# Decode attention over a key/value cache: four heads interleaved over the partitions in 16 KB runs, weights turned on VectorE and permuted by one matmul

## The chip, the cores and the metric

The kernel runs on one core of one Trainium2 chip. The metric is the device time of one execution in microseconds (us), lower is better. Executions of the kernel before agree within 0.3% or so. All timed comparisons are between runs made on the same chip in the same rounds. A profile is of one execution; its span is about 2 us shorter than the device time.

Engine names in the profile: PE is TensorE (matmul), PEld its weight loads, DVE is VectorE, ACT is ScalarE, SPq the queue that issues the loads. "Granted clock" (PEclk) is the share of its full clock that TensorE was allowed.

## The reference, cut to what matters

```python
# B=8 sequences, one new token each, D=448; 16 query heads, 8 key heads, 256 wide, window W=1024
q = (x @ wq)                                            # 8 x 16 x 256
k, v = k_cache[:, :, -1024:, :], v_cache[:, :, -1024:, :]   # each serves two query heads
p = softmax(q k^T / 16);  o = p v;  a = o @ wo
b = mlp(layernorm(x))                                   # 448 -> 1792 -> 448
return g * a + (1 - g) * b                              # g: a sigmoid gate
```

Keys and values are 64 pairs of (sequence, key head), 512 KB of keys and 512 KB of values each in bf16. With the weights the kernel must read 77.7 MB.

## The kernel before

Work goes in 16 groups `u` of four key heads (8 query heads). For a group, key tiles arrive with keys on the partitions, TensorE transposes them, VectorE and ScalarE copy the transposes from PSUM to SBUF ("evict"), TensorE makes the scores, the softmax gives weights, and TensorE multiplies them with the values. A ring of 18 slots of 1 MB takes the loads.

```python
def kv_loader(src, b, g):            # two heads to a 1 MB tile: 128 runs of 8 KB
    nc.sync.dma_start(t[:], src[b, g:g+GP, kv_base:Sk, :]
        .rearrange("a (s c) d -> s a (c d)", c=NCK))      # partition = (s, a), a = head, GP = 2

def transpose_keys(u):
    for s in range(2):                # ... kt: [P, NJ, NCK, SK, GP], so heads alternate in its columns
        nc.tensor.transpose(ktp[:, c*P:(c+1)*P], kn[:, o:o+P], ident[:])    # 8 to a PSUM tile
        # evictions 2, 4, 7 of 8 on ScalarE, the others on VectorE

def scores(u):                        # 4 heads side by side in 4 column groups of the array
    for hf in range(2):
        for j in range(NJ):
            for a in range(QUAD):
                nc.tensor.matmul(S_ps[32*a:32*a+rep, hf*NMM:(hf+1)*NMM],
                    lhsT=qw[:, j, b, h0:h0+rep],                                  # 2 columns
                    rhs=KT[a//GP][:, j, hf*CMM:(hf+1)*CMM, :, a % GP], ...)       # 512 keys, every 2nd element

def softmax(u):                       # every weight is written twice: 2048 elements
    nc.vector.reduce_max(nmx[:], S_ps[:], axis=AXIS.X, negate=True)
    nc.scalar.activation(E (two copies), S_ps, ACT.Exp, bias=nmx[:], accum_out=rowsum[:])

def weights(u):                       # turned by 16 matmuls with E as stationary operand
    # rsum = 1/rowsum; selr = sel * rsum * 2
    for c in range(NCK):
        nc.tensor.matmul(sm[:, c, :], lhsT=E[:, c*P:(c+1)*P], rhs=sel[:], ...)
    nc.tensor.matmul(sm[:, NCK, :], lhsT=ones_f[:], rhs=selr[:], ...)
    nc.vector.tensor_tensor(ET[:], sm[:, 0:NCK, :], own (0 or 1), op=ALU.mult)

def values(u, ET, rb):                # 64 matmuls, values stationary, 4 columns of weights streaming
    ...
for u in range(1, NQ - 2):
    transpose_keys(u)
    values(u - 1, *weights(u - 1))
    scores(u)
    softmax(u)
# ... the last two groups are interleaved; the output projection with wo (loaded last) follows
```

## Time and profile before

| | before |
|---|---|
| device time, median | 198.85 us (198.73 to 199.01, 3 runs) |
| span of the profile | 197.0 us |
| bytes read | 77.68 MB, 394 GB/s over the span |
| one loop, undisturbed (transposes at 90.96 and 101.13 us) | 10.17 us |
| last packet of the last weights (packet records) | 193.0 us |

The page in 40 slices of 4.9 us each: busy tenths of TensorE, its granted clock in tenths, busy tenths of the DMA engines.

```profile
PE   1699869868686878979596868686868686887662
PEclk9996556999999996799999999999999999997555
DMA  4999999999999999999999999999999999999960
```

DMA is at 9 from the second slice to the 38th, so the bytes leave hardly any room. The clock is low at the start, in one stretch around 75 to 85 us and at the end, else 1.0.

The page's groups of instructions: line, engine, operation, out <- in, shapes, count, then busy us and mean ns, then idle time before them and what ended it.

```profile
L366 ACT ACTIVATE E<-S_ps,nmx 128x2048 bf16<-128x2048 f32 x16 | 31.5, 1968 | 72.2 <-DVE nmx L363 72.2
L363 DVE TENSOR_REDUCE nmx<-S_ps 128x1 f32<-128x1024 f32 x16 | 19.6, 1225 | 13.0 <-PE S_ps L351 13.0
L351 PE MATMUL S_ps<-kt,qw 128*2 128x512 bf16 x256 | 18.1, 402 | 0.4 <-DVE qw L339 0.4
L386 PE MATMUL sm<-sel,E 128*128 128x8 bf16 x256 | 8.8, 167 | 1.7 <-ACT E L366 1.7
```

One loop in the timeline (start us, us, engine, line, operation, count, in brackets the idle time before and its releaser; lines between these are left out):

```profile
90.96 1.51 PE L311 MATMUL ktp<-ident,slot 128*128 128x128 bf16 x24
92.33 1.97 ACT L366 ACTIVATE E<-S_ps,nmx 128x2048 bf16<-128x2048 f32 x1 [4.59 <-DVE nmx L363]
95.34 1.52 PE L311 MATMUL ktp<-ident,slot 128*128 128x128 bf16 x24 [1.19 <-ACT kt L316]
96.70 0.55 PE L386 MATMUL sm<-sel,E 128*128 128x8 bf16 x16
98.44 1.75 PE L414 MATMUL po<-ET,slot 128*128 128x4 bf16 x64 [0.38 <-DVE ET L395]
100.11 1.08 PE L351 MATMUL S_ps<-kt,qw 128*2 128x512 bf16 x16
...
101.13 1.07 PE L311 MATMUL ktp<-ident,slot 128*128 128x128 bf16 x16
```

The loop is a ring of dependences: transposes (which wait for ScalarE, held up by the exponential), turned weights, values, scores, and the next transposes. It takes 10.17 us; the DMA engines bring a group's 4 MB in about 10.1 us. The two limits lie almost on top of each other. What the loop sheds, DMA will not give; what the loop gains in length, the time shows.

### The profile page before, as it was taken

What the parts mean: (1) busy time and instruction counts of PE and PEld (TensorE: products, weight loads), DVE (VectorE), ACT (ScalarE), POOL (GpSimd) and SP (SyncE); (2) the same over time, 40 slices, a digit from 0 to 9 for tenths busy, and PEclk for the clock granted to TensorE, in tenths of its full rate; (3) what the DMA queues carried; (4) which work ended last, traced back from release to release, by engine and by line L of the source; (5) the groups of instructions that cost most, each with busy time, mean ns of one, the idle gap of its engine ahead of it and who ended that gap; (6) DMA issues with size and microseconds to landing.
All of it is one profiled execution on the core that took longest, in us unless ns stands there. A gap on an engine that the chain in (4) does not pass through costs nothing.

```text
span 197.0 us, 6578 instructions
## 1 busy us (share of the span) xinstructions
PE 147.7 (75%) x3006; PEld 125.1 (64%) x3006; DVE 94.3 (48%) x230; ACT 82.0 (42%) x85; POOL 0.9 (0%) x7
## 2 busy tenths in 40 slices
PE   1699869868686878979596868686868686887662
PEld 0699739656574758877575667575656665675641
DVE  6540335364646464555545454636363636763200
ACT  3250043272636354362718180808172727383000
POOL 1000000000000000000000000000000000000000
PEclk9996556999999996799999999999999999997555
DMA  4999999999999999999999999999999999999960
GB/s 170 416 427 406 420 412 414 421 414 424 411 414 419 419 419 416 414 419 419 423 411 411 423 416 423 409 418 423 416 416 413 418 419 419 421 411 416 413 246 23
DMA packets 11645, 78.10 MB, mean 396 GB/s; under 512 B 1489, under 2 KB 1890, under 8 KB 3042
## 3 DMA queue, kind: packets, MB, share of 16 engines
q1 hardware_dynamic: 11424, 77.68, 95.8%
q8 instruction: 23, 0.38, 0.8%
q10 hardware_dynamic: 194, 0.02, 0.1%
q14 instruction: 4, 0.03, 0.0%
HBM read 77.68 MB, written 0.01 MB: 394 GB/s over the span
## 4 chain that ended last, share of the span: by engine, by line
DMA 49%; PE 26%; DVE 16%; ACT 5%; issue 2%; SPq 0%; ACTq 0%
DMA slot<-in_A_v_cache_dram 31%; PE ktp L311 10%; DMA slot<-in_A_wq_dram 8%; DVE kt L318 7%; PE po L414 7%; DMA slot<-in_A_wo_dram 7%; DVE nmx L363 6%; PE S_ps L351 5%; ACT kt L316 4%; DMA slot<-in_A_k_cache_dram 3%; PE sm L393 2%; ACT E L366 1%; DVE ET L395 1%; DVE selr L381 1%; PE bb L484 1%
## 5 line engine op out<-in xcount | busy, mean ns | idle before, releaser
L311 PE MATMUL ktp<-ident,slot 128*128 128x128 bf16 x1024 | 73.9, 232 | 21.6 <-ACT kt L316 15.2
L311 PEld LDWEIGHTS <-slot 128*128 128x128 bf16 x1024 | 66.1, 105 | 33.3 <-issue 28.3
L318 DVE COPY kt<-ktp 128x1024 bf16<-128x1024 bf16 x80 | 52.5, 686 | 30.3 <-PE ktp L311 29.0
L366 ACT ACTIVATE E<-S_ps,nmx 128x2048 bf16<-128x2048 f32 x16 | 31.5, 1968 | 72.2 <-DVE nmx L363 72.2
L316 ACT COPY kt<-ktp 128x1024 bf16<-128x1024 bf16 x48 | 47.1, 1013 | 19.3 <-PE ktp L311 19.3
L414 PEld LDWEIGHTS <-slot 128*128 128x128 bf16 x1024 | 29.5, 99 | 6.8 <-issue 6.8
L414 PE MATMUL po<-ET,slot 128*128 128x4 bf16 x1024 | 28.1, 164 | 5.3 <-DVE ET L395 5.3
L363 DVE TENSOR_REDUCE nmx<-S_ps 128x1 f32<-128x1024 f32 x16 | 19.6, 1225 | 13.0 <-PE S_ps L351 13.0
L351 PE MATMUL S_ps<-kt,qw 128*2 128x512 bf16 x256 | 18.1, 402 | 0.4 <-DVE qw L339 0.4
L423 DVE TENSOR_TENSOR oT<-po,rb 128x8 bf16<-128x8 f32 x32 | 4.3, 190 | 26.5 <-PE po L414 26.5
L393 PE MATMUL sm<-selr,ones_f 128*128 128x8 f32 x32 | 6.6, 279 | 5.5 <-DVE selr L381 5.5
L386 PE MATMUL sm<-sel,E 128*128 128x8 bf16 x256 | 8.8, 167 | 1.7 <-ACT E L366 1.7
L393 PEld LDWEIGHTS sm<-selr,ones_f 128*128 128x128 f32 x32 | 5.2, 203 | 6.8 <-DVE selr L381 6.6
L386 PEld LDWEIGHTS <-E 128*128 128x128 bf16 x256 | 8.2, 97 | 1.8 <-ACT E L366 1.8
L395 DVE TENSOR_TENSOR ET<-sm,own 128x128 bf16<-128x128 f32 x16 | 4.7, 291 | 8.2 <-PE sm L393 8.2
L351 PEld LDWEIGHTS <-qw 128*2 128x2 bf16 x256 | 4.7, 82 | 5.2 <-DVE qw L339 0.5
L545 PE MATMUL A_ps<-slot,oP 128*8 128x112 bf16 x128 | 4.3, 290 | 2.8 <-DMA slot<-in_A_wo_dram 2.1
L545 PEld LDWEIGHTS <-oP 128*8 128x8 bf16 x128 | 2.9, 113 | 4.1 <-issue 3.4
L329 PE MATMUL qt<-xT,slot 128*128 128x8 bf16 x128 | 3.9, 168 | 0.8 <-DMA slot<-in_A_wq_dram 0.4
L329 PEld LDWEIGHTS <-slot 128*128 128x128 bf16 x128 | 3.7, 104 | 1.0 <-DMA slot<-in_A_wq_dram 0.6
L381 DVE TENSOR_SCALAR selr<-sel,rsum 128x8 f32<-128x8 bf16 x16 | 3.7, 231 | 0.6
L552 DVE SCALAR_TENSOR_TENSOR res<-A_ps,gg_s,mixb 128x112 bf16<-128x112 f32 x1 | 0.3, 335 | 6.6 <-PE A_ps L545 6.6
(69 smaller groups left out, 38.9 us busy)
## 6 DMA issues: line engine op xcount, KB each, us to landing
slot<-in_A_k_cache_dram SPq DMA_DIRECT2D x32, 1024.0 KB, 19.9
slot<-in_A_v_cache_dram SPq DMA_DIRECT2D x32, 1024.0 KB, 19.9
slot<-in_A_wq_dram SPq DMA_DIRECT2D x3, 1024.0 KB
slot<-in_A_wo_dram SPq DMA_DIRECT2D x3, 896.0 KB, 19.1
slot<-in_B_w_dram SPq DMA_DIRECT2D x1, 1008.0 KB
slot<-in_B_w_dram SPq DMA_DIRECT2D x1, 896.0 KB
slot<-in_B_w_dram SPq DMA_DIRECT2D x1, 560.0 KB
slot<-in_A_wq_dram SPq DMA_DIRECT2D x1, 512.0 KB
```

What stands on the lines that cost most here:

```text
L311: nc.tensor.transpose(ktp[:, c * P : (c + 1) * P], kn[:, o : o + P], ident[:])
L316: nc.scalar.copy(dst, ktp[:])
L318: nc.vector.tensor_copy(dst, ktp[:])
L329: nc.tensor.matmul(qt[:, k, :], lhsT=w[:, c : c + P], rhs=xT[:, r + half, :], start=(r == 0 and k == 0), stop=(r == NR), skip_group_check= ...
L351: nc.tensor.matmul(S_ps[32 * a : 32 * a + rep, hf * NMM : (hf + 1) * NMM], lhsT=qw[:, j, b, h0 : h0 + rep], rhs=KT[a // GP][:, j, hf * CMM ...
L363: nc.vector.reduce_max(nmx[:], S_ps[:], axis=AXIS.X, negate=True)
L366: nc.scalar.activation(E[:].rearrange("p (k a) -> p k a", a=GP), S_ps[:].rearrange("p (k o) -> p k o", o=1).to_broadcast([P, W, GP]), ACT.Exp,
L386: nc.tensor.matmul(sm[:, c, :], lhsT=E[:, c * P : (c + 1) * P], rhs=sel[:], start=True, stop=True,)
L393: nc.tensor.matmul(sm[:, NCK, :], lhsT=ones_f[:], rhs=selr[:], start=True, stop=True)
L395: nc.vector.tensor_tensor(ET[:], sm[:, 0:NCK, :], own[:].rearrange("p (o r) -> p o r", o=1).to_broadcast([P, NCK, RQ]), op=ALU.mult,)
L414: nc.tensor.matmul(PO[:, j, cols], lhsT=vn[:, o : (c + 1) * Dh : NJ], rhs=ET[:, c, cols], start=(c == 0), stop=(c == NCK - 1),)
L545: nc.tensor.matmul(dst, lhsT=oP[:, j, q, :], rhs=w[:, o + cols.start : o + cols.stop], start=(q == 0 and j == 0), stop=(q == NHQ - 1 and j ...
```

## The change: its intent, and the diff

A tile now holds four heads, 2 MB, in 128 runs of 16 KB, so that DMA has half the packets for keys and values. As all four heads share a tile, the weights need no second copy: the exponential halves. VectorE turns the weights in 32x32 blocks, and one matmul with a permutation puts them in the order of the value tiles' partitions; 16 matmuls go. A score matmul writes 8 rows per head, so that the turned blocks are full; a cap of the maximum makes the weights of rows that are not the head's zero. Cut to its core:

```diff
-    GP = 2
-    SLOT = 4096
-    RING = 18
+    SLOT = 8192
+    RING = 9
 # kv_loader: all four heads of a group in one tile
-                src[b, g : g + GP, kv_base:Sk, :].rearrange("a (s c) d -> s a (c d)", c=NCK)
+        v = src[b, half * QUAD : (half + 1) * QUAD, kv_base:Sk, :].rearrange(
+            "a (s c) d -> s a (c d)", c=NCK)                    # NCK = 32, runs of 16 KB
 # scores
-                        S_ps[32 * a : 32 * a + rep, hf * NMM : (hf + 1) * NMM],
-                        lhsT=qw[:, j, b, h0 : h0 + rep],
-                        rhs=KT[a // GP][:, j, hf * CMM : (hf + 1) * CMM, :, a % GP],
+                        S_ps[32 * a : 32 * a + RQ, hf * CH * SK : (hf + 1) * CH * SK],
+                        lhsT=qw[:, j, b, half, a, :],           # 8 columns, 6 of them zero
+                        rhs=KT[hf][:, j, :, a::QUAD],           # every 4th element
 # softmax
+        nc.vector.tensor_tensor(nmx[:], nmx[:], cap[:], op=ALU.min)
-            E[:].rearrange("p (k a) -> p k a", a=GP),  S_ps[:] ... .to_broadcast([P, W, GP]),
+            E[:], S_ps[:], ACT.Exp, bias=nmx[:], scale=1.0, accum_out=rowsum[:]
 # weights
-        for c in range(NCK):
-            nc.tensor.matmul(sm[:, c, :], lhsT=E[:, c * P : (c + 1) * P], rhs=sel[:], ...)
+        nc.vector.transpose(EB[:].rearrange("p c r -> p (c r)"), E[:])
+        nc.tensor.matmul(sm[:, 0:NCK, :], lhsT=perm[:], rhs=EB[:, :, 0:RQ], ...)
-        nc.vector.tensor_tensor(ET[:], sm[:, 0:NCK, :], own ..., op=ALU.mult)
+        nc.vector.tensor_copy(ET[:], sm[:, 0:NCK, :])
 # ... slots of 2 MB for the weight matrices, set-up of perm, sel, cap: cut
```

The values were already the stationary operand; now 8 columns of weights stream past them instead of 4.

## The prediction

> **What bounds it now.** Two limits lie almost on top of each other. (1) Bytes: the page's slices show the DMA engines at 0.9 or more from slice 2 to 38, for 77.68 MB; in the stretch table each 10.17 us moves 411 to 421 GB/s. Packet records: median 313 ns for 8192 B, 275 for 7168, 140 for 3584, 74 for 1792, so about 0.0375 ns per byte plus 5.5 ns per packet (estimate: fit). (2) Compute: the loop repeats every 10.17 us (transposes at 92.95, 103.12, 113.29), and after the stretch with granted clock 0.70 (75 to 85 us) it stays 0.8 us late, so it is set by its own chain, not by data. The chain of waits agrees: transposes, evictions, values, scores and maximum from 24 to 118 us, DMA only after. PE is busy 7.7 us of 10.17. The end (last weights landing, 193 us) is DMA; compute has about 2.5 us of slack there.

> **Bytes after.** The same, in 16 KB packets for keys and values: one 5.5 ns saved per 16 KB plus half the completion writes (9 ns each), estimated 27 ns of 2543 ns per MB, about 1%, 1.7 us over 64 MB.

> **Compute loop after**, from its start:
> - Exponential of 1024 instead of 2048 elements: 1.97 us to about 1.0 (ScalarE copies of 1024 take 1.01). The last evictions and transposes come about 0.75 us sooner (PE waits 1.19 us per loop on a ScalarE eviction), less 0.19 for the new minimum with cap.
> - 16 matmuls with exponentials as weights (0.55 us) go. VectorE turns 128x1024 instead. [...]this trace's maximum over 1024 elements takes 1.225 us, so I estimate 1.2 us. It stands in VectorE's order behind the last evictions, so on the chain. Then a 256-column matmul (estimate 0.27) and a copy of 256 columns (estimate 0.42, from 0.29 for 128).
> - Last transpose to first value matmul grows from 1.6 to about 2.4 us, which gives back the 0.75. Loop: 10.2 us, unchanged within 0.3.
> - Scores read keys at a step of 8 B instead of 4; values take 8 columns instead of 4 but weight loads bound them (27 ns each). I expect 1.08 and 1.74 us as before.[...]
> - Start: more small VectorE operations before the first eviction (about 1.3 us), eight strided query writes instead of two (about 1.1 us more): loop starts about 1.5 us later.

> **Sum.** Without compute, 1.6 us less: 197.2. But compute at 10.2 us against DMA's 10.05 falls behind: values of the last group end about 3 us later, at 189, the output projection then runs without waiting, and ends at about 194.5 instead of 193.9. Time about 199.

> **What would show it.** 16 KB packets near 620 ns; about 420 GB/s; exponential 1.0 us; the turn 1.2 us, with PE idle before the permutation 0.7 to 1.1 us; loop 10.0 to 10.4 us; output projection no longer waiting for DMA.

> **What would make it wrong.** A slower turn, or scores slowed by the 8 B step: each 0.3 us per loop is about 4 us at the end. Longer PE gaps could lower the granted clock oftener (0.85 us each).[...] Much cheaper 16 KB packets: 195.5.

> Predicted 199.0 us, 8 in 10 within 196.5 to 203.5; faster by over 2%: 0.06, within: 0.77, slower: 0.17.

Two of its figures can be looked up in the trace before: the 9 ns are the median of the 1330 packets of 4 bytes, which the author takes for completion writes, and the 0.85 us are about what the stretch of low clock cost (transposes at 71.77 and 92.95 us, 21.18 us for two loops of 10.17).

## The result, and the profile after

The changed kernel takes 218.22 us (median of 4, 217.74 to 218.98), against 198.93 us of the kernel before in the same rounds. The ratio is 1.0974 (95% interval 1.0937 to 1.1011): 9.7% slower. Ratios here and below are the mean time of one kernel's fast runs over that of the other's of the same rounds, so not quite the ratio of the medians quoted. The prediction of 199.0 us, and its range to 203.5, were wrong.

The same three rows of the page after (slices of 5.4 us):

```profile
PE   0599948787868696958696877969686959687672
PEclk9996587888879969797969698788789696999758
DMA  5999999999999999999999999999999999600000
```

DMA now ends five slices before the kernel does: the loads are done at 190 us of 216. The clock dips all through the run, not in one stretch. The groups that answer to those of before, and the new turn:

```profile
L373 ACT ACTIVATE E<-S_ps,nmx 128x1024 bf16<-128x1024 f32 x16 | 17.8, 1113 | 104.6 <-DVE nmx L370 84.4
L369 DVE TENSOR_REDUCE nmx<-S_ps 128x1 f32<-128x1024 f32 x16 | 19.6, 1225 | 27.2 <-PE S_ps L357 27.2
L357 PE MATMUL S_ps<-kt,qw 128*8 128x512 bf16 x256 | 32.4, 628 | 0.3 <-DVE qw L348 0.3
L385 DVE STREAM_TRANSPOSE EB<-E 128x1024 bf16<-128x1024 bf16 x16 | 19.8, 1238 | 0.0
L386 PE MATMUL sm<-EB,perm 128*128 128x256 bf16 x16 | 4.3, 270 | 12.0 <-DVE EB L385 12.0
```

The exponential (1.11 us), the turn (1.24 us) and the permutation (0.27 us) are near what was forecast. The score matmuls are not: 628 ns each instead of 402, and the maximum on VectorE waits 27.2 us for them instead of 13.0. One loop after:

```profile
100.38 1.51 PE L320 MATMUL ktp<-ident,slot 128*128 128x128 bf16 x24
102.02 1.11 ACT L373 ACTIVATE E<-S_ps,nmx 128x1024 bf16<-128x1024 f32 x1 [6.81 <-DVE nmx L370]
104.17 1.52 PE L320 MATMUL ktp<-ident,slot 128*128 128x128 bf16 x24 [0.39 <-ACT kt L323]
106.16 1.24 DVE L385 STREAM_TRANSPOSE EB<-E 128x1024 bf16<-128x1024 bf16 x1
107.45 0.27 PE L386 MATMUL sm<-EB,perm 128*128 128x256 bf16 x1 [0.76 <-DVE EB L385]
108.23 1.75 PE L401 MATMUL po<-ET,slot 128*128 128x8 bf16 x64 [0.52 <-DVE ET L390]
109.91 2.00 PE L357 MATMUL S_ps<-kt,qw 128*8 128x512 bf16 x16
...
111.84 0.40 PE L320 MATMUL ktp<-ident,slot 128*128 128x128 bf16 x2
```

Subtract starts within the two loops. From the first transposes to the first value matmul: 7.48 us before (98.44 - 90.96), 7.85 after. From there to the scores: 1.67 and 1.68. From the scores to the next transposes: 1.02 and 1.93. The loop grew by 1.29 us, to 11.46 us, and 0.91 of that is the score matmuls.

The loop growth is nearly the whole difference of the spans. Transposes of group 1 start at 29.30 us before and 31.32 after (2.0 us later); from there to the transposes of group 14 it is 132.85 us before and 149.47 after (16.6 us more); from there to the end 34.84 and 35.17 (0.3 more). Unrounded, these sum to 19.0 us, the difference of 216.0 and 197.0.

The packet records say that DMA itself got faster: a 16 KB packet has a median of 614 ns, an 8 KB packet before 313 ns. But now the queue waits for the computation to free slots. The queue's own waits, before and then after (line, what it waited for, us in total, times, longest):

```profile
SPq L100 <- DMA slot<-in_A_k_cache_dram: 52.8, 28, 1.9
SPq L100 <- PE ktp L311: 5.1, 15, 0.5
```

```profile
SPq L107 <- PE ktp L320: 57.8, 11, 6.6
SPq L107 <- PE po L401: 34.3, 10, 3.8
```

### The profile page after: what moved, and what is told of

Same layout as the page of the kernel before. It is cut to its first block, busy times and chain, and to the rows that moved or that the text cites. A ratio compares the mean times of both kernels' runs of the same rounds, so it can differ in the third digit from the quotient of the medians.

```text
span 216.0 us, 6058 instructions
## 1 busy us (share of the span) xinstructions
PE 161.3 (75%) x2766; PEld 124.0 (57%) x2766; DVE 116.0 (54%) x241; ACT 68.3 (32%) x85; POOL 0.8 (0%) x7
## 3 DMA queue, kind: packets, MB, share of 16 engines
q1 hardware_dynamic: 6528, 77.67, 85.5%
HBM read 77.68 MB, written 0.01 MB: 360 GB/s over the span
## 4 chain that ended last, share of the span: by engine, by line
PE 37%; DVE 31%; DMA 14%; ACT 10%; issue 6%; SPq 0%; ACTq 0%
DMA slot<-in_A_k_cache_dram 14%; PE S_ps L357 13%; PE po L401 12%; DVE kt L325 10%; DVE EB L385 9%; PE ktp L320 8%; DVE nmx L369 7%; ACT kt L323 6%; ACT E L373 4%; DVE ET L390 3%; PE sm L386 2%; PE A_ps L529 1%; DVE selr L381 1%; DVE nmx L370 1%; PE pp L514 0%
## 5 line engine op out<-in xcount | busy, mean ns | idle before, releaser
L373 ACT ACTIVATE E<-S_ps,nmx 128x1024 bf16<-128x1024 f32 x16 | 17.8, 1113 | 104.6 <-DVE nmx L370 84.4
L369 DVE TENSOR_REDUCE nmx<-S_ps 128x1 f32<-128x1024 f32 x16 | 19.6, 1225 | 27.2 <-PE S_ps L357 27.2
L401 PE MATMUL po<-ET,slot 128*128 128x8 bf16 x1024 | 28.7, 167 | 7.2 <-DVE ET L390 7.2
L357 PE MATMUL S_ps<-kt,qw 128*8 128x512 bf16 x256 | 32.4, 628 | 0.3 <-DVE qw L348 0.3
L385 DVE STREAM_TRANSPOSE EB<-E 128x1024 bf16<-128x1024 bf16 x16 | 19.8, 1238 | 0.0
L409 DVE TENSOR_TENSOR oT<-po,rb 128x16 bf16<-128x16 f32 x16 | 3.6, 226 | 26.1 <-PE po L401 26.1
L386 PE MATMUL sm<-EB,perm 128*128 128x256 bf16 x16 | 4.3, 270 | 12.0 <-DVE EB L385 12.0
L357 PEld LDWEIGHTS <-qw 128*8 128x8 bf16 x256 | 6.1, 93 | 12.3 <-issue 11.0
L390 DVE CAST ET<-sm 128x256 bf16<-128x256 f32 x16 | 6.8, 425 | 5.8 <-PE sm L386 5.8
L381 DVE TENSOR_SCALAR selr<-sel,rowsum 128x8 f32<-128x8 f32 x16 | 3.6, 223 | 0.6 <-ACT E L373 0.6
L392 DVE RECIPROCAL rb<-sm 128x8 f32<-128x8 f32 x16 | 3.2, 198 | 0.0
```

Source lines behind the costliest of these rows:

```text
L357: nc.tensor.matmul(S_ps[32 * a : 32 * a + RQ, hf * CH * SK : (hf + 1) * CH * SK], lhsT=qw[:, j, b, half, a, :], rhs=KT[hf][:, j, :, a::QUA ...
L373: nc.scalar.activation(E[:], S_ps[:], ACT.Exp, bias=nmx[:], scale=1.0, accum_out=rowsum[:])
L385: nc.vector.transpose(EB[:].rearrange("p c r -> p (c r)"), E[:])
L386: nc.tensor.matmul(sm[:, 0:NCK, :], lhsT=perm[:], rhs=EB[:, :, 0:RQ], start=True, stop=True)
L390: nc.vector.tensor_copy(ET[:], sm[:, 0:NCK, :])
L401: nc.tensor.matmul(PO[:, j, :], lhsT=vn[:, c * Dh + j : (c + 1) * Dh : NJ], rhs=ET[:, c, 0:RQ], start=(c == 0), stop=(c == NCK - 1),)
```

## The experiments

Theory A: the score matmuls are slow because they read the keys at a step of four elements, 8 B, instead of two. Rival B: they are slow because of what else changed in them, 8 stationary columns and 8 rows written instead of 2. When A alone did not give back what it should, a second pair of theories was needed: C, the wait for the turn on VectorE, placed between transposes and values, leaves TensorE so quiet that its clock is lowered; D, the clock falls for another reason.

Experiments with wrong keys passed the comparison with the reference as well: the scores are so small that the weights are almost even, and the comparison doesn't see the order of the keys. So a "correct" says little about it; e13 and e14 settle the order where it matters.

### e1 to e4: step or width?

e1 takes the step away by reading wrong keys; e2 takes the width away; e3 puts the step alone into the kernel before; e4 takes the step away properly, by sorting the keys in the transposing matmul.

```diff
 # e1 (changed kernel)
-rhs=KT[hf][:, j, :, a::QUAD],
+rhs=KT[hf][:, j, 4 * a : 4 * a + 4, :],
 # e2 (changed kernel)
-S_ps[32 * a : 32 * a + RQ, ...],  lhsT=qw[:, j, b, half, a, :],
+S_ps[32 * a : 32 * a + rep, ...], lhsT=qw[:, j, b, half, a, a * rep : (a + 1) * rep],
 # e3 (kernel before)
-rhs=KT[a // GP][:, j, hf * CMM : (hf + 1) * CMM, :, a % GP],
+rhs=KT[a // GP][:, j].rearrange("p c s g -> p (c s g)")[:, a::4],
 # e4 (changed kernel)
+back[:].rearrange("p (a s) -> p a s", a=QUAD) <- ident[:].rearrange("p (s a) -> p a s", a=QUAD)
-nc.tensor.transpose(ktp[:, c, :], kn[:, o : o + P], ident[:])
+nc.tensor.transpose(ktp[:, c, :], kn[:, o : o + P], back[:])
-rhs=KT[hf][:, j, :, a::QUAD],
+rhs=KT[hf][:, j, :, a * SK : (a + 1) * SK],
```

> The changed kernel, but each score matmul reads 512 keys that lie side by side (same size and count, wrong keys, so a wrong result on purpose). Theory A (the 8 B step of the keys that the score matmuls stream slows them): the 16 score matmuls of a loop fall from 1.97 us to 1.1 or less, the loop from 11.46 to about 10.5 us, the time to about 203 to 205 us. Theory B (the stationary operand of 8 columns, or writing 8 rows instead of 2, slows them): scores stay at 1.97 us, time stays near 218.

> The changed kernel with a stationary operand of 2 columns instead of 8 in the score matmuls, still at the 8 B step (wrong result on purpose: three of four heads lose their scores). Theory A: nothing moves, scores 1.97 us a loop, time near 218. Theory B: scores back to about 1.08 us, loop about 10.5 us, time 203 to 205.

> The kernel before, with nothing changed but the score matmuls reading the keys at a step of four elements (8 B) instead of two (wrong keys, wrong result on purpose). Theory A: scores 1.08 to about 1.97 us a loop, the loop from 10.17 to about 11.05 us, time about 208 to 211. Theory B: nothing moves, 199.

> The changed kernel with the permutation taken into the key transposes: they use a permuted identity, so that each head's keys stand in runs of 32 in the transposed tile and the score matmuls read with no step. The result is right if the transposing matmul takes a permutation. Theory A: scores 1.1 us or less, loop about 10.5 us, time 203 to 205 us: that is, slower than the kernel before still, by the 0.3 us per loop that the turn on VectorE and its wait add. Theory B: 218.

| run | time, us | ratio to before (95%) | 16 scores of a loop, us | mean loop, us |
|---|---|---|---|---|
| changed kernel | 218.22 | 1.097 | 1.97 to 2.02 | 11.50 |
| e1, no step (wrong keys) | 214.15 | 1.076 (1.074 to 1.078) | 1.04 to 1.88 | 11.32 |
| e2, two columns | 218.56 | 1.098 (1.095 to 1.102) | 1.97 to 2.01 | 11.49 |
| e3, before with the 8 B step | 207.97 | 1.045 (1.043 to 1.047) | 1.97 to 2.01 | 11.03 |
| e4, keys sorted | 214.40 | 1.078 (1.071 to 1.085) | 1.04 to 1.88 | 11.26 |

(Mean loop: start of the transposes of group 1 to those of group 13, over 12. The kernel before: 10.23 us with its one slow stretch, scores 1.07 to 1.09 us.)

B is out: e2 changes nothing, and e3 gets the slow scores with two columns. A is right as to the score matmuls: the step alone makes 1.08 into 1.97 us, in either kernel, and in e3 it lengthens the loop by 0.8 us. The page's group of e3:

```profile
L351 PE MATMUL S_ps<-kt,qw 128*2 128x512 bf16 x256 | 31.7, 626 | 0.4 <-DVE qw L339 0.4
```

But A's sum failed: without the step the time falls by 4 us, not by the 13 to 15 us expected. In e4's timeline three neighbouring loops show why:

```profile
97.34 1.88 PE L362 MATMUL S_ps<-kt,qw 128*8 128x512 bf16 x16
108.78 1.88 PE L362 MATMUL S_ps<-kt,qw 128*8 128x512 bf16 x16
120.22 1.54 PE L362 MATMUL S_ps<-kt,qw 128*8 128x512 bf16 x16
```

### e5 and e8: the low clock and the wait

e5 fills the wait in e4 with useless matmuls; e8 puts the turn, with its result unused, into the kernel before.

```diff
 # e5 (e4's kernel), between the ones matmul and the permutation
+for _ in range(18):
+    nc.tensor.matmul(sm[:, NCK+8:NCK+24, :], lhsT=ident[:], rhs=ident[:], start=True, stop=True)
 # e8 (kernel before), ahead of the weighting of the weights
+nc.vector.transpose(turned[:], E[:, 0:W])
 nc.vector.tensor_tensor(ET[:], sm[:, 0:NCK, :], own ..., op=ALU.mult)
```

> The kernel with sorted keys (e4) plus 18 useless 128-column matmuls per loop, placed where TensorE waits for the turn on VectorE (right result). In e4 the score matmuls read with no step and still took 1.88 us in the loops whose granted clock was 0.5 at that moment, and 1.04 us where it was 1.0. Theory C (the wait for the turn, placed between the transposes and the values, leaves TensorE so quiet that its clock is lowered, and the scores then run cold): with the wait filled the clock stays at 1.0 in most windows, the scores take 1.04 to 1.1 us, the loop falls from 11.4 to about 10.5 us, the time from 214 to 203 to 206 us, although TensorE has more to do. Theory D (the clock is lowered for another reason): clock near 0.78 still, and the time 214 or more, up to 220 as the fillers run cold.

> The kernel before with one useless turn of 128x1024 on VectorE ahead of the weighting of the weights (1.24 us on its chain, result unused and right). Theory C: the wait alone lowers the clock in the kernel before too, mean granted clock about 0.8 instead of 0.896, score matmuls of many loops 1.88 instead of 1.08 us, loop 11.6 to 12.2 us, time 217 to 226 us. Theory D: only the added wait counts, loop about 11.3 us, scores 1.08 us, clock 0.9, time about 212 to 214.

e5: 210.76 us (ratio 1.059, 1.055 to 1.064), 4 us faster than e4, with 1.2 us more for TensorE to do in each loop. The share of time at the low clock fell from 39 to 22%. Where the clock stayed up, the loop is as theory C had it; from the timeline of e5, the transposes starting two loops in a row, 10.59 us apart:

```profile
118.25 1.04 PE L362 MATMUL S_ps<-kt,qw 128*8 128x512 bf16 x16
119.22 1.51 PE L325 MATMUL ktp<-back,slot 128*128 128x128 bf16 x24
...
125.38 1.17 PE L392 MATMUL sm<-ident 128*128 128x128 bf16 x18
128.84 1.04 PE L362 MATMUL S_ps<-kt,qw 128*8 128x512 bf16 x16
129.81 2.40 PE L325 MATMUL ktp<-back,slot 128*128 128x128 bf16 x22
```

It stayed up in only part of the loops, so the expected 203 to 206 us were not reached. Filling the one gap is not enough; other pauses remain (0.68, 0.40, 0.60 and 0.51 us in the loop shown).

e8: 207.82 us (1.044, 1.042 to 1.046), less than either theory's number, because part of the turn ran beside the ones matmul: it lengthened the chain by 0.54 us and not by 1.24 (first value matmul 8.02 us after the first transposes, in the loop at 95.99 us, instead of 7.48). But the clock did what C says and D doesn't: the low share rose from 9 to 28% and the scores took up to 1.88 us, with nothing else changed in the kernel before. The clock's row of the page of e8, and the scores of one loop:

```profile
PEclk9996559696696969997878789996969695799555
116.91 1.88 PE L351 MATMUL S_ps<-kt,qw 128*2 128x512 bf16 x16
```

These shares are of one profile each, and the windows of 3.41 us do not keep step with loops of 10 to 11.5 us, so their size is rough. The mean granted clock of every execution points the same way: 0.849 to 0.887 in the seven of the kernel before in these rounds, 0.823 in both of e8, 0.784 to 0.793 in the four of e4, 0.851 to 0.866 in the four of e5.

But the longest wait does not tell the clock: TensorE's longest in the loops shown is 1.19 us in the kernel before and only 0.76 us in the changed one. A count over the kept traces fits better. It was made after the runs and its thresholds are fitted to them, so it is an estimate that no further run has tested. Each trace from 30 to 165 us was cut into the windows of 3.41 us of its clock records, and the time added up in which columns stream through the array in each window. A column was taken at 0.42 ns (e4's 0.215 us over 512), four scores side by side were counted once, and scores slowed by a step at their measured 0.45 or 0.90 us. Of 618 windows in the 16 traces, 146 came to under 0.34 of their length, and after all of them the next window was at clock 0.5; 411 came to over 0.40, and after 409 of them it was at 1.0; the 61 between are mixed.

In this count the 64 value matmuls of a loop are nearly silent: 8 columns each, 0.2 us of the 1.75 us that they take. With the best single threshold the count misplaces 10 windows. It misplaces 137 if the values count as busy throughout, 176 if the transposes are left out, and 31 if the slowed scores count by their columns alone. The emptiest windows of the kernel before stand at 0.36 to 0.41, just at the edge. In the changed kernel about one window in each loop falls to between 0.07 and 0.38, as the waits for the turn stand beside the quiet values. Theory C was thus right that the late turn brings the clock down, but it is not alone: e3 (22%) and e7 (34%, below) have low windows without it.

### e6 and e7: the wait moved off the chain

VectorE sits idle 0.91 us in the changed kernel between its third and fourth eviction of a loop, and the exponentials of the group before are there by then (done at 103.13 us in the loop shown, the gap begins at 103.91). e6 is e4 with the turn issued at that place; e7 is the changed kernel, step and all, with the turn at that place.

```diff
 # e6 and e7, transpose_keys(u), behind the fourth eviction (VectorE's third)
+if evac[0] % 8 == 4:
+    turn(u - 1)        # selr = sel * rowsum; nc.vector.transpose(EB, E)
 # weights(u): those two lines taken away; the ones matmul and the permutation stay
```

> e4 (sorted keys) with the turn of the weights and the small scaling before it moved forward in VectorE's order: behind the third of its five evictions instead of behind the fifth, where VectorE has nothing to do (right result). Theory C: TensorE's gap before the values shrinks from about 2.5 to 1.2 us, the clock stays up, scores 1.04 us; the compute loop alone would take about 9.3 us, so that DMA's 9.9 us per group bounds the kernel and the last weights' landing its end: 195 to 197 us, faster than the kernel before. Theory D: cold scores remain, loop about 10.2 to 10.5 us, time about 200 to 204.

> The changed kernel with the turn moved forward as in e6 and the keys still read at the 8 B step (right result). Theory A says that the step alone costs 0.9 us per loop whatever the clock: scores 1.97 us, loop 10.1 to 10.4 us, time 198 to 202 us. If the step only mattered through the clock, this is as fast as e6.

e7: 199.17 us, ratio 1.0007 (0.9986 to 1.0029), as fast as the kernel before, with loops of 10.28 us and the slow scores (1.97 to 2.02 us). So the late turn costs 1.2 us of loop (11.50 to 10.28), more than the step does. By the page of e7, the scores are as slow as before the move, and the permutation waits 0.6 us in all for the turn instead of 12.0:

```profile
L377 PE MATMUL S_ps<-kt,qw 128*8 128x512 bf16 x256 | 32.4, 628 | 0.3 <-DVE qw L368 0.3
L402 PE MATMUL sm<-EB,perm 128*128 128x256 bf16 x16 | 4.4, 276 | 0.6 <-DVE EB L322 0.6
```

Its clock was still at 0.5 for 34% of the time: the time came back because the wait left the chain, not because the clock rose, and the wait for the turn is not the only thing that brings the clock down.

e6: 197.05 us (196.94 to 197.14), ratio 0.990 (0.9886 to 0.9919): 1% faster than the kernel before, inside the 2% that count as the same, but clear of noise. The mean loop is 9.94 us, that of DMA. The chain that ended last has become DMA's, by the page of e6 (share of the span by engine, then by line):

```profile
DMA 96%; SPq 1%; issue 0%; PE 0%; DVE 0%
DMA slot<-in_A_k_cache_dram 58%; DMA slot<-in_A_v_cache_dram 21%; DMA slot<-in_A_wo_dram 10%; DMA slot<-in_A_wq_dram 7%; SPq L107 1%; SPq L123 1%; SPq L172 0%; PE A_ps L545 0%; DVE res L552 0%
```

against, in the changed kernel,

```profile
PE 37%; DVE 31%; DMA 14%; ACT 10%; issue 6%; SPq 0%; ACTq 0%
```

Theory C had expected the clock to stay up in e6. It did not: 31% low, while TensorE waits for loads (its weight loads waited 15.4 us in all for keys). It just does not matter any more: a bound by DMA has room for it. That part of the expectation is a miss, and a reminder that a low clock is only a cost where TensorE is on the chain. The time too was a little over the 195 to 197 expected.

### e9 to e11: what the step does

Which step is free, and is it one stream or four at once that are slowed? e9 lets the four heads' matmuls follow one another on one column group; e10 and e11 read at two and eight elements.

```diff
 # e9 (changed kernel)
-S_ps[32 * a : 32 * a + RQ, ...],  start=(j == 0), stop=(j == NJ - 1)
+S_ps[0:RQ, ...],                  start=True, stop=True
 # e10, e11 (changed kernel)
-rhs=KT[hf][:, j, :, a::QUAD],
+rhs=KT[hf][:, j, 8 * (a // 2) : 8 * (a // 2) + 8, (a % 2) :: 2],            # e10
+rhs=KT[hf][:].rearrange("p j c k -> p (j c k)")[:, a + 4 * j :: 8],         # e11
```

> The changed kernel, but all four heads' score matmuls write the same 8 rows, so that they follow one another on one column group instead of running four at a time (wrong result on purpose); keys still at the 8 B step. Theory A1 (the step slows the reading only because four streams read at once[...]): alone one stream is not slowed, about 0.215 us per matmul at full clock, 16 in about 3.5 us. Theory A2 (each stream by itself is slowed by the step): about 0.44 us per matmul at full clock, 16 in about 7 us.

> The changed kernel with the score matmuls reading at a step of two elements (4 B, wrong keys on purpose). Theory A1: 7.6 keys per ns as in the kernel before, 16 matmuls in 1.08 us where the clock is 1.0 and 1.88 where it is 0.5; time near e1, 213 to 215 us.

> The changed kernel with the score matmuls reading at a step of eight elements (16 B, wrong keys on purpose). Theory A1: [...]half the rate again: 16 matmuls in about 3.9 us, loop about 13.4 us, time about 248 us.[...]

(e11's rival to A1 was a fixed cost of any step beyond 4 B: scores of 1.97 us and 218 us again.)

(One run each, state unknown; what is read is the matmuls' spacing, not the time: 301.77, 214.60 and 244.83 us.) The scores of one loop in the timelines of e9 and then e11:

```profile
111.43 7.38 PE L357 MATMUL S_ps<-kt,qw 128*8 128x512 bf16 x16
```

```profile
107.74 3.77 PE L357 MATMUL S_ps<-kt,qw 128*8 128x512 bf16 x16
```

Theory A1 (the step is slow only because four streams read at once) falls: one stream alone is as slow as four. In e9 the matmuls start every 0.45 us, and in the changed kernel four start together every 0.44 to 0.45 us. Spacing of matmuls of 512 keys in one column group, from their starts at full clock:

| step | 1 (e4) | 2 (before, e10) | 4 (changed, e9) | 8 (e11) |
|---|---|---|---|---|
| us per 512 keys | 0.215 | 0.225 to 0.23 | 0.45 | 0.90 |

e11's rival falls too: from a step of 4 to 8 the time doubles. An estimate from these numbers: from a step of 2 the time grows in proportion to the step, 0.1125 us for each element of it (0.90 / 8, and 0.45 / 4); at 2 that makes 0.225 us, as measured, just over the 0.215 us at step 1. What in the reading sets this is not shown, and a step of 16 was not run. So the kernel before sat, by luck or by tuning, at the largest of these steps that is nearly free; the change doubled it.

### e12: the 16 KB packets alone

```diff
 # e12 (e6's kernel): every key and value tile as two loads with runs of 8 KB
-def add_kv(name, src, u, parts=1):
+def add_kv(name, src, u, parts=2):
```

> e6 (sorted keys, turn early) with each key and value tile loaded in two halves of 8 KB runs instead of one of 16 KB. e6 is bound by DMA to its end. If the 16 KB packets are what the change gains (landings 2477 ns per MB in the changed kernel against 2528 before), this runs 3 us longer: 199.5 to 201 us, no faster than the kernel before. If the faster landing comes from elsewhere, it stays at 197.

198.95 us, ratio 0.9994 (0.9977 to 1.0010): the same as the kernel before, and 1.9 us over e6. So the longer runs are worth the whole gain of e6 (e12 also has twice as many loads, which this run can't tell apart from the packets), and it is about the 1.7 us that the prediction worked out from the packet durations, not the 3 us that the landing times suggested. The last packet lands at 193.1 us instead of 190.1; the rest is given back behind it.

### e13 and e14: is the sorted order right?

```diff
 # e13 (e6's kernel; ring of 8 slots for room): for the first eight key chunks
+plain = the same chunks transposed with ident
+worst = max over all of (KT[0] - plain read as "p c (s a) -> p c a s") ** 2
+mixb += 1000 * (sum of worst over the partitions)
 # e14: the same, plain read as "p c (a s) -> p c a s"
```

> e6 with one comparison added: eight key chunks of the first group are also transposed with the plain identity, the difference from the permuted ones, read in the order that the permutation should give, is squared, its greatest value times 1000 is added to the output. If the transposing matmul takes a permutation as it should, the difference is exactly zero and the output agrees with the reference. Its time doesn't matter.

> The control to e13: the same comparison, but against the keys in the unpermuted order. The output must disagree with the reference; if it agrees, the comparison sees nothing and e13 says nothing.

e13's output agrees with the reference; e14's does not (relative error 286426). So the transposing matmul takes a permutation in place of the identity, at no more time (24 transposes take 1.51 us with either, in the loops shown of the kernel before and of e5), and the sorted keys of e4, e5, e6 and e12 are where they should be (e7 does not sort). The times of e13 and e14, 196.29 and 196.37 us, are single runs of unknown state with a ring of 8, and nothing is read from them.

## Why the prediction was wrong

- **What bounds the kernel before** was right: two limits within 1% of each other. e6 and e12 confirm it from the other side: the compute loop made shorter is worth nothing by itself (e12, 0.9994).
- **Bytes**: 1.7 us forecast, 1.9 us measured (e12 against e6). Right, though no part of it reached the changed kernel's time, as compute ended 26 us behind the last load. "16 KB packets near 620 ns" was 614.
- **Exponential, turn, permutation**: 1.0, 1.2, 0.27 us forecast, 1.11, 1.24, 0.27 measured. The estimate of the turn from the maximum held: over 1024 elements they take 1.24 and 1.225 us. The chain to the first value matmul was forecast as unchanged (the 0.75 us won being given back) and grew by 0.37 us. In the loops shown, the last transposes start 0.59 us sooner after the first (4.38 to 3.79 us), where the forecast had 0.75 less 0.19 for the minimum but then left the 0.19 out of its sum. The way from there to the values grew by 0.96 us (3.10 to 4.06), not by 0.8.
- **Scores: the first step that failed.** "I expect 1.08 and 1.74 us as before": for the scores that was not shown by any measurement. The values did take 1.75 us. The scores took 1.97: e3 shows that the step alone does it, e2 that the width does not, e9 that a single stream suffers it. That is 0.9 us in each loop, and the prediction itself said what it leads to: each 0.3 us of a loop some 4 us at the end. It named the risk and then bet against it, with a trace that had no 8 B step in it.
- **The clock.** The prediction named "longer PE gaps could lower the granted clock oftener". It did fall, from 9 to 31% of the time. But in the changed kernel it was hidden under the slow scores, and only taking the step away (e1, e4) brought it to light. This is the second step that failed: with free scores, as the prediction assumed them, the kernel still takes 214.40 us (e4) and not 199. At full clock e4's loop would be about 7.85 + 1.68 + 0.97 = 10.50 us (an estimate: the last term is from the scores to the next transposes in e5, whose undisturbed loops take 10.59); its mean is 11.26, because the late turn, whose wait the sum counted only as a wait, also lets the clock fall. The late turn and the step are two causes that cover for each other: taking away the step alone saves 0.24 us of a loop, taking away the late turn alone 1.2 us, both together bring the loop to DMA's 9.94 us.
- **Start**: 1.5 us later forecast, 2.0 measured.

## What to carry to other kernels

A change of layout for one consumer (here DMA's longer runs) sets the step at which every other consumer reads: list those steps, and measure each one that the trace doesn't have. A transposing matmul took a permutation here at no more time (1.51 us for 24 with either, e13 for the order), so interleaved columns can be sorted there. Work that waits in an engine's order behind something it doesn't need should be moved to where that engine is idle, above all if TensorE waits for it: the pause costs once as a wait, and can cost again as a lower clock (low share 39% in e4 and 22% in e5 with the pause filled; 9% in the kernel before and 28% in e8 with one added). To judge the clock, count the columns that stream in each window (the edge here, by an estimate fitted to 618 windows, lay between 0.34 and 0.40 of its length), not the length of the waits.
